# A fused retention and two-layer kernel: another order of products where two stages meet, keys and values loaded by pairs of batches, weights and queries requested later

## The chip, the core and the metric

One Trainium2 chip, one of its cores. The core has a matrix engine (TensorE: PE in the profile, and PEld for its weight loads), a vector engine (DVE), an activation engine (ACT), GpSimd (POOL), and SyncE (SP), which here only issues DMA requests, in program order, each after its own wait. The metric is the device time in microseconds of one execution. The kernel before takes 644.52 us (median of 4 runs, 644.33 to 644.72).

## What is computed

```python
# q, k, v: (4 batches, 8 heads, 768 tokens, 64), fp32
for t in range(S):
    state = gamma * state + outer(k[t], v[t])       # per batch and head
    y[t] = scale * q[t] @ state
x = y as (3072, 512)
h = x @ w_in                                        # 512 -> 2048
out = max(0.01 * h, h) @ w_out                      # 2048 -> 512
```

The recurrence is computed by chunks of 128 tokens: products inside a chunk (scores of queries and keys, masked, times values) and products of the queries with the state that is carried over. w_in and w_out arrive as 64-bit numbers and are turned into fp32 on ACT and DVE.

## The kernel before

There are NC = 6 chunks `c` of 4 batches `b`. The hidden dimension is cut into NU = 4 units `u`. For a chunk and a unit, `hidden` makes h and `output` adds its part of the result; both are done with seven block products instead of eight (M1 to M7), whose sums and differences are formed on DVE and copied on ACT. Each of the M products is a step of a generator (`seven`), so that other work can be put between two steps: `products(steps, n)` runs n of them.

The program has three parts. Chunks 0 and 1 are computed while the 64 weight pieces are still being loaded and converted (up to about 203 us of the trace). The last four raw pieces (60 to 63) lie in the two slots of the tag `qk` (60 and 62) and the two of `kv` (61 and 63); a slot can be loaded anew when DVE has read its piece. Meanwhile sums of the unit tiles are formed and stored to DRAM (`keep_unit`, line 1017, tensor `kept`). A middle part (lines 1059 to 1092) places the first visits of chunk 2 by hand among the steps of chunk 1. Then comes the main loop over n = 0 to 15, that is chunks 2 to 5 with four units each. There each chunk's inputs are treated once more by seven products: `inner` (line 1154) computes one unit's products in two groups, group 0 with the streamed weights `wa` and group 1 with `wb`, each a single buffer that `load_unit` (lines 1044 to 1049) fills from `kept`.

`inner` runs M1, M5, M4, M6, M2, M3, M7 (line 1163) in four banks of PSUM. M6 and M7 go to the bank that ACT fills with a copy of M1 (line 1167), so M6 waits for that copy; M3 goes to the bank of M5 and waits for its copy (line 1169); M7 waits for the copy of M6 (line 1173). `outer` (group 1) adds the parts on DVE (line 592) and applies the leaky function on ACT, four instructions (line 1198), each after its sum.

Two of the four iterations of a chunk hold a visit of the next chunk, for two batches at a time. `scores_of_pair` computes scores of queries and keys (line 357), then products of keys and values for the state (line 368). `joint_visit` computes the products of queries and state (line 413) and of weights and values (line 430). Before that, `decay_v` on POOL (line 142) multiplies the values by the powers of gamma.

Who loads what, on SP, in order:

- `end_mantissas`, after the last piece: `load(2, 0)`, `load(2, 1)`; each asks for queries with keys of a batch (line 121, 512 KB), then for keys and values (line 137, 512 KB).
- `next_heads`, after the visit of chunk 2: for each of two batches queries, then values, then keys (line 314, 256 KB each).
- `joint_visit`: values of two batches, keys of two batches, then `ahead`, the queries of the chunk after; and behind it `load_unit(n + 2, 0)`, the next `wa`.

A tile named `kv` of one batch holds keys and values side by side; the tag has two slots (`AHEAD = 2`), so a pair of batches uses both until its `joint_visit` has read the values.

The order where the middle part meets the main loop is written out at lines 1232 to 1245: the last output of chunk 1 is a generator `last` of seven steps, and `last` M1, M5, M6, M2; the scores of (3, 0); `last` M7; `inner(0, 0)`, `outer(0, 0)`; `last` M3 and M4; `inner(0, 1)`, `outer(0, 1)`; and the loop begins with `differences` (DVE) and `inner(1, 0)`.

Of the kernel before, what the change touches and what calls it, by code (L numbers as in the profile page):

```python
# [22 lines left out]
def kernel(  # L23
# [82 lines left out]
    def place_for(c, b, place=None):  # L106

        if place is None:
            x = work.tile([128, 2, HP, C], FP32, tag="qk", bufs=AHEAD, name=f"qk_{c}_{b}")
            y = work.tile([128, 2, H, D], FP32, tag="kv", bufs=AHEAD, name=f"kv_{c}_{b}")  # L110
        else:
            flat = place.rearrange("p i k n -> p (i k n)")
            half = 2 * HP * C
            if place.shape[1] == 7:
                rooms[b] = flat[:, 2 * half : 2 * half + 2 * HP * D]
            x = flat[:, 0:half].rearrange("p (s a t) -> p s a t", s=2, a=HP)
            y = flat[:, half : 2 * half].rearrange("p (s h d) -> p s h d", s=2, h=H)
        heads[c, b] = x, y
# [7 lines left out]
    def load_k(c, b):  # L126
        nc.sync.dma_start(out=heads[c, b][1][:, 0], in_=kv[c, b][:, 0])

    rooms = {}

    def spare(b):
        return lambda: rooms[b].rearrange("p (n a d) -> p n a d", n=2, a=HP)

    def load(c, b, place=None):
        place_for(c, b, place)
# [1 line left out]
        nc.sync.dma_start(out=heads[c, b][1], in_=kv[c, b])  # L137

    def decay_v(c, b, engine=nc.gpsimd):
        v = heads[c, b][1][:, 1]  # L140
        if engine is not nc.scalar:
            engine.tensor_tensor(out=v, in0=v,
                                 in1=gk[c].unsqueeze(2).to_broadcast([128, H, D]), op=ALU.mult)
        else:
            for h in range(H):
                engine.activation(v[:, h], v[:, h], AF.Identity, scale=gk[c][:, h : h + 1])
# [148 lines left out]
    def ahead(c, b):  # L295

        if c >= NC:
            return
        if b < 2:
            x = work.tile([128, 2, HP, C], FP32, tag="qk", bufs=AHEAD, name=f"qk_{c}_{b}")  # L300
        else:
            if b == 2:
                room[c] = new_o(0).rearrange("p i k n -> p (i k n)")
            x = room[c][:, ds((b - 2) * 2 * HP * C, 2 * HP * C)]
            x = x.rearrange("p (s a t) -> p s a t", s=2, a=HP)
        heads[c, b] = [x, None]
        load_qk(c, b)

    def load_kv(c, b, kinds):
        if heads[c, b][1] is None:  # L310
            heads[c, b][1] = work.tile([128, 2, H, D], FP32, tag="kv", bufs=AHEAD,
                                       name=f"kv_{c}_{b}")
        for i in kinds:
            nc.sync.dma_start(out=heads[c, b][1][:, i], in_=kv[c, b][:, i])

    room = {}

# [26 lines left out]
    def scores_of_pair(c, b, banks=None, mid=None):  # L344

        if b == 0 and c > JOINED:
            next_gq()
        banks = banks or bank
        at = [banks[j].rearrange("p (b m i t) -> p b m i t", b=2, m=HP // 2, i=2)
              for j in range(2)]  # L350
        sums = [banks[2 + h].rearrange("p (b a d) -> p b a d", b=2, a=HP) for h in range(2)]
        for n in range(2):
            x = heads[c, b + n][0]
            for m, i, a in quads:
                for h in range(2):
                    for j in range(2):
                        nc.tensor.matmul(at[j][ts(h, 64), n, m, i],  # L357
                                         lhsT=x[ts(j, 64), 1, a, ts(h, 64)],
                                         rhs=x[ts(j, 64), 0, a, ts(h, 64)],
                                         start=(n == 0 and a == 0), stop=True,  # L360
                                         skip_group_check=True)
        last = c == NC - 1
        for n in range(2):
            y = heads[c, b + n][1]
            for a in range(HP):
                for j in range(2):
                    for h in range(1 if last else 2):
                        nc.tensor.matmul(sums[h][ts(j, 64), n, a], lhsT=y[ts(h, 64), 0, 2 * a + j],  # L368
                                         rhs=y[ts(h, 64), 1, 2 * a + j],
                                         start=(n == 0 and a == 0), stop=True,  # L370
                                         skip_group_check=True)
        weights = scores[c, b] = []
        for j in range(2):
            am = work.tile([128, 2, HP // 2, 2, C // 2], FP32, tag=f"am{j}", name=f"am{j}_{c}_{b}")
            nc.vector.tensor_tensor(
                out=am.rearrange("p b m i t -> p (b m i) t"),
                in0=at[j].rearrange("p b m i t -> p (b m i) t"),
                in1=mask[:, 0].unsqueeze(1).to_broadcast([128, 2 * HP, C // 2]), op=ALU.mult)
            weights.append(am)
        p = b // 2  # L380
        old = state_of[p]
        free_again[p] = [old]
        if mid is None:
            mid = halves_of_states.pop(0)
            free_again[p].append(mid)
        plus(mid, old, sums[0])
        if not last:
            state_of[p] = halves_of_states.pop(0)
            plus(state_of[p], mid, sums[1])
        mid_of[p] = old, mid  # L390

    def rows_free(mm):

# [4 lines left out]
    def joint_visit(c, b, banks=None):  # L398
# [23 lines left out]
            return mm  # L422

        def value(n, crossed, after=None):
            y = heads[c, b + n][1]
            for m in range(HP // 2):
                for i in range(2):
                    for j in range(2):
                        h, a = j ^ crossed, 2 * m + i
                        mm = nc.tensor.matmul(at[n][j][ts(i, 64), m, ts(h, 64)],  # L430
                                              lhsT=y[ts(h, 64), 1, 2 * a + j],
                                              rhs=weights[j][ts(h, 64), n, m, i],
                                              start=(n == 1 and crossed == 1 and m == 0),
                                              stop=True, skip_group_check=True)
# [20 lines left out]
        for n in range(2):  # L455
            heads.pop((c, b + n))
        if later is not None:
            for n in range(2):
                load_kv(later[0], later[1] + n, (1,))
            for n in range(2):  # L460
                load_kv(later[0], later[1] + n, (0,))
            for n in range(2):
                decay_v(later[0], later[1] + n)
        for n in range(2) if c > JOINED else ():
            ahead(c + 1, b + n)

    def pair_of_banks(name):

# [65 lines left out]
    def end_mantissas():  # L534
# [4 lines left out]
            load_piece(n + 4 if n < 3 else n + 3)  # L539
        if n == N_PIECES - 1:  # L540
            new_pair(2)
            for b in range(AHEAD):
                load(2, b)
        if n % 4 == 3 and n > 7:
            add_sums(n // 4)

# [487 lines left out]
    def at_of(n):  # L1034
        return 2 + n // NU, n % NU
# [21 lines left out]
        load_unit(0, 1)  # L1057

    def next_heads():
        for b in range(2):  # L1060
            ahead(3, b)
            load_kv(3, b, (1, 0))
        for b in range(2):
            decay_v(3, b)

# [2 lines left out]
        (1, 1): dict(s2=[sum_of_unit(0, 2)], s5=[sum_of_unit(0, 3)]),  # L1068
        (0, 2): dict(s2=[sum_of_unit(1, 2)], s5=[sum_of_unit(1, 3)]),
        (1, 2): dict(s0=[keep_unit(1)], s2=[sum_of_unit(2, 0)]),  # L1070
        (0, 3): dict(s0=[lambda: load(2, 3, place_of_unit(2, "in23"))],
                     s4=[lambda: load(2, 2, place_of_unit(0, "in22"))],
                     s5=[sum_of_unit(3, 0)], s6=[sum_of_unit(3, 1), early_decays(2, 2)]),
        (1, 3): dict(s0=[begin_x(2), early_scores(2, 2, spare(3))],
                     s1=[sum_of_unit(3, 2)], s2=[sum_of_unit(3, 3)],
                     s3=[keep_unit(3)], s4=[early_visit(2, 2)],
                     s6=[early_decays(2, 0)]),
# [4 lines left out]
        (1, 1): dict(s6=[sum_of_unit(1, 1)]),  # L1082
        (0, 2): dict(s2=[sum_of_unit(2, 1)], s5=[sum_of_unit(2, 2)]),
        (1, 2): dict(s0=[sum_of_unit(2, 3)], s1=[keep_unit(2)]),
        (0, 3): dict(s0=[begin_units, early_scores(2, 0, spare(2))],
                     s1=[lambda: differences(*parts[1][1:])],
                     s3=[early_visit(2, 0), differ(2), next_heads],
                     s6=[sums(2, 0)]),
# [64 lines left out]

    def inner(n, group, held=False):

        c, u = at_of(n)
        w, count = streamed[group], 4 - group
        moving = operands(c, group)
# [2 lines left out]
        for m, q, j, s in INNER:  # L1161
# [16 lines left out]
            elif m == "M7":  # L1178
                plus(sums[:, 3], sums[:, 3], ps[3])
                plus(sums[:, 2], sums[:, 2], ps[3])  # L1180
        if not held:
            load_unit(n + 1, group)

# [54 lines left out]
    sums_of_x(2, 1)  # L1238
    inner(0, 0)
    outer(0, 0)  # L1240
    products(last, 2)
    inner(0, 1)
    outer(0, 1)

    for n in range(N2):
# [7 lines left out]
        if n + 1 < N2 and u == NU - 1:  # L1253
            sums_of_x(c + 1, 1)
        if n + 1 < N2:
            inner(n + 1, 0, held=visiting)
            outer(n + 1, 0)
        if visiting and u == 0:
            xs[c + 1] = new_x(c + 1)
        if visiting:  # L1260
            joint_visit(c + 1, 2 * u)
            load_unit(n + 2, 0)
        steps = output(c, os[c], [gs.pop(n)], u == 0, u == NU - 1, room=room if more else last_room,
                       order=FUSED if more else LAST)
        products(steps, 3)
        if c + 1 < NC and u < 2 and following(c + 1, 2 * u):
            scores_of_pair(*following(c + 1, 2 * u))
        products(steps, 1)
        if c + 1 < NC and u == 1:
            differences(*xs[c + 1])  # L1270
# [1 line left out]
            sums_of_x(c + 1, 0)  # L1272
        if more:
            inner(n + 1, 1)
            products(steps, 1)
            outer(n + 1, 1)
        if n + 2 == N2:
# [29 lines left out]
def _layout(q, k, v, w_in, w_out):  # L1307
# [15 lines left out]

    qk = np.stack([dims_first(q), dims_first(k)], axis=3).reshape(NC, B, 2 * D, 2, HP, C)
    kv = np.stack([tokens_first(k), tokens_first(v)], axis=3).reshape(NC, B, C, 2, H, D)
    DM, DF = w_in.shape

    w_in = w_in.reshape(H // 4, 2, 2, D, DF).transpose(2, 0, 1, 3, 4).reshape(DM, DF)
# [41 lines left out]
```

## Time and profile before

| | us |
|---|---|
| median of 4 runs | 644.52 (644.33 to 644.72) |
| profiled execution, its own time | 644.45 |
| its span, first to last instruction | 642.7 |
| PE busy | 633.0 (98%) |
| DVE busy | 460.9 (72%) |
| ACT busy | 269.5 (42%) |
| POOL busy | 22.2 (3%) |
| mean granted clock of TensorE | 0.997 |
| chain that ended last, on PE | 94% |
| longest groups on PE: line 648, bank from g and w | 89.9 |
| line 1163, bank from x and wb | 77.9 |

The span is 1.75 us shorter than the execution's own time; what lies outside it is taken as fixed. The "chain of work" view goes back from the last instruction to whatever released each step. The "timeline" view gives start, duration, engine, line, tiles and, in brackets, the idle time before an instruction and what ended it. In the DMA view of a stretch, the first row gives the busy share of the 16 DMA engines in 40 slices, the second what they moved.

### The profile page before, as it was taken

The page shows a single profiled execution, that of the slowest core. Times are in us where ns is not written, and L with a number is a line of the kernel's source. Part 1 is how long each engine was busy: PE and PEld are TensorE (multiplying, and loading weights), DVE is VectorE, ACT ScalarE, POOL GpSimd, SP SyncE. Part 2 cuts the span into 40 slices and gives each one's busy share as a digit, 9 for nine tenths or more (in the row PEclk, how much of TensorE's full clock was granted, in tenths as well). Part 3 has the DMA queues.
Part 4 walks back from the last instruction along what each step waited for, and adds up shares of the span by engine and source line. Part 5 has one row for each costly group of instructions (what it writes and reads, how often), then busy time and mean ns, then how long its engine had stood idle before and what let it go on. Part 6 is the DMA issues. An engine that isn't in the chain of part 4 may idle for free.

```text
span 642.7 us, 14314 instructions
## 1 busy us (share of the span) xinstructions
PE 633.0 (98%) x6086; PEld 571.4 (89%) x6086; DVE 460.9 (72%) x760; ACT 269.5 (42%) x515; POOL 22.2 (3%) x45
## 2 busy tenths in 40 slices
PE   8999999999999998999999999999999999999997
PEld 5888888888888887998999999999999999999996
DVE  5689769889979967466876746768637778637656
ACT  5876557257252134252342433523424323433521
POOL 2000000000011010101000001000010000000000
PEclk9999999999999999999999999999999999999999
DMA  8931327455964977547544584645455336545201
GB/s 335 406 116 47 117 66 244 137 196 153 309 252 134 339 292 234 182 152 248 153 134 135 191 276 130 204 157 160 152 183 188 98 115 188 165 145 172 86 1 67
DMA packets 89265, 113.43 MB, mean 176 GB/s; under 512 B 3432, under 2 KB 71912, under 8 KB 89200
## 3 DMA queue, kind: packets, MB, share of 16 engines
q1 hardware_dynamic: 88896, 111.88, 53.1%
q8 instruction: 48, 0.79, 0.5%
q10 hardware_dynamic: 304, 0.62, 0.3%
q14 instruction: 17, 0.14, 0.1%
HBM read 93.35 MB, written 19.14 MB: 175 GB/s over the span
## 4 chain that ended last, share of the span: by engine, by line
PE 94%; DMA 2%; ACT 1%; DVE 1%; issue 0%; SPq 0%; POOL 0%; DVEq 0%; POOLq 0%
PE bank L648 31%; PE bank L1163 27%; PE C_h L648 4%; PE A_h L648 4%; PE C_o L648 4%; PE A_o L648 4%; PE B_h L648 4%; PE B_o L648 4%; PE D_o L648 2%; PE D_h L648 2%; PE d L669 2%; DMA kv<-in_kv_dram 1%; PE bank L430 1%; PE bank L413 1%; PE bank L368 1%; PE bank L357 1%
## 5 line engine op out<-in xcount | busy, mean ns | idle before, releaser
L592 DVE TENSOR_TENSOR made<-made,bank 128x512 f32<-128x512 f32 (+1 forms) x96 | 56.4, 618 | 62.1 <-PE bank L1163 57.6
L592 DVE TENSOR_TENSOR o<-o,bank 128x512 f32<-128x512 f32 (+2 forms) x91 | 58.6, 661 | 53.7 <-PE bank L648 32.9
L648 PE MATMUL bank<-g,w 128*128 128x256 f32 x384 | 89.9, 382 | 0.0
L1163 PEld LDWEIGHTS bank<-x,wb 128*128 128x128 f32 x672 | 77.6, 192 | 1.6 <-issue 0.8
L648 PEld LDWEIGHTS bank<-g,w 128*128 128x128 f32 x384 | 70.7, 190 | 9.2
L1163 PE MATMUL bank<-x,wb 128*128 128x128 f32 x672 | 77.9, 275 | 0.6 <-issue 0.6
L1163 PE MATMUL bank<-x,wa 128*128 128x128 f32 x512 | 69.6, 278 | 2.9 <-ACT bank L1167 2.9
L1163 PEld LDWEIGHTS bank<-x,wa 128*128 128x128 f32 x512 | 64.4, 193 | 4.7 <-ACT bank L1167 3.9
L648 PE MATMUL bank<-gd,w 128*128 128x256 f32 x288 | 66.1, 379 | 0.0
L648 PEld LDWEIGHTS bank<-gd,w 128*128 128x128 f32 x288 | 54.7, 190 | 7.4
L1163 PE MATMUL bank<-t,wa 128*128 128x128 f32 x384 | 54.5, 279 | 0.0
L1198 ACT ACTIVATE g<-g 128x512 f32<-128x512 f32 x64 | 39.4, 631 | 34.2 <-DVE g L592 34.2
L1163 PEld LDWEIGHTS bank<-t,wa 128*128 128x128 f32 x384 | 49.2, 196 | 0.0
L1167 ACT COPY bank<-bank 128x512 f32<-128x512 f32 (+1 forms) x32 | 16.7, 522 | 66.4 <-PE bank L1163 66.1
L592 DVE TENSOR_TENSOR g<-made 128x512 f32<-128x512 f32 x64 | 42.7, 688 | 1.2
L741 ACT COPY bank<-bank 128x512 f32<-128x512 f32 x17 | 9.7, 570 | 72.6 <-PE bank L648 72.5
L595 DVE TENSOR_TENSOR gd<-g,gd 128x512 f32<-128x512 f32 x48 | 33.2, 692 | 4.9
L759 ACT COPY bank<-bank 128x512 f32<-128x512 f32 x16 | 9.1, 570 | 47.0 <-PE bank L648 47.0
L648 PE MATMUL bank<-g,last 128*128 128x256 f32 x120 | 28.3, 380 | 0.0
L648 PE MATMUL bank<-gd,last 128*128 128x256 f32 (+1 forms) x124 | 27.5, 373 | 0.0
L648 PE MATMUL A_h<-x,w 128*128 128x256 f32 x112 | 26.6, 380 | 0.0
L648 PEld LDWEIGHTS bank<-gd,last 128*128 128x128 f32 x124 | 22.9, 190 | 3.3 <-DVE gd L595 0.3
(222 smaller groups left out, 1027.4 us busy)
## 6 DMA issues: line engine op xcount, KB each, us to landing
wa<-kept SPq DMA_DIRECT2D x16, 1344.0 KB, 7.8
raw<-in_weights_dram SPq DMA_DIRECT2D x31, 512.0 KB, 4.3
wb<-kept SPq DMA_DIRECT2D x16, 896.0 KB, 5.3
kv<-in_kv_dram SPq DMA_DIRECT2D x28, 256.0 KB, 4.7
wa<-kept SPq DMA_DIRECT2D x16, 448.0 KB, 5.2
wb<-kept SPq DMA_DIRECT2D x16, 448.0 KB, 6.1
out_dram<-o SPq DMA_DIRECT2D x23, 256.0 KB, 3.9
kept<-w SPq DMA_DIRECT2D x12, 448.0 KB, 6.2
```

Of the source, the lines that this page charges most:

```text
L357: nc.tensor.matmul(at[j][ts(h, 64), n, m, i], lhsT=x[ts(j, 64), 1, a, ts(h, 64)], rhs=x[ts(j, 64), 0, a, ts(h, 64)], start=(n == 0 and a = ...
L368: nc.tensor.matmul(sums[h][ts(j, 64), n, a], lhsT=y[ts(h, 64), 0, 2 * a + j], rhs=y[ts(h, 64), 1, 2 * a + j], start=(n == 0 and a == 0), s ...
L413: mm = nc.tensor.matmul(at[n][j][ts(i, 64), m, ts(h, 64)], lhsT=by_half[h][ts(j, 64), n, a], rhs=x[ts(j, 64), 0, a, ts(h, 64)], start=(n = ...
L592: nc.vector.tensor_tensor(out=out, in0=a, in1=b, op=ALU.add)
L595: nc.vector.tensor_tensor(out=out, in0=a, in1=b, op=ALU.subtract)
L648: nc.tensor.matmul(to, lhsT=block(w, sa)[:, k, ts(i, 128)], rhs=rhs[:, k, a:z], start=(first and (i == 0 or split) and n == 0 and k == 0), ...
L669: nc.tensor.matmul(banks[r][:, i, :], lhsT=block(2 * u, r + 2 * kh)[:, k, ts(i, 128)], rhs=x[:, 2 * kh + th, k, :], start=(step == 0 and i ...
L741: nc.scalar.copy(out=bank_of("B"), in_=ps)
L759: nc.scalar.copy(out=bank_of("D"), in_=ps)
L1163: nc.tensor.matmul(ps[q][:, i], lhsT=w[:, j, i], rhs=part_of(moving[i], s), start=(i == 0 and m in ("M1", "M5", "M4")), stop=True, skip_gr ...
L1167: nc.scalar.copy(out=ps[3], in_=ps[0])
L1198: nc.scalar.activation(g[:, i], g[:, i], AF.Prelu, alpha=0.01)
```

## The change

Three things are done. First, keys and values of chunks 2 to 5 lie differently in DRAM (a host-side reordering) and come in two loads for a pair of batches, one of the values and one of the keys, each of 512 KB, into tiles of their own (`of_pair`). The keys of the pair after are requested at the end of `scores_of_pair`, the values still in `joint_visit`. Second, requests change their order: after the last piece, values and keys of (2, 0) and (2, 1) come first, then the two loads of queries; `next_heads` does the same for chunk 3; in the loop `load_unit(n + 2, 0)` comes behind `scores_of_pair`, and `ahead` behind `inner(n + 1, 1)`. Third, at the junction `last` M4 moves behind `inner(0, 1)`, and the first step of `inner(1, 0)` with its copy is issued ahead of `outer(0, 1)`; the other steps stay behind `differences`.

```diff
+    def of_pair(c, b, kind, place=None):
+        if place is None:
+            place = work.tile([128, 2, H, D], FP32, tag="kv", bufs=AHEAD,
+                              name=f"{'kv'[kind]}_{c}_{b}")
+        for n in range(2):
+            (keys, vals)[kind][c, b + n] = place[:, n]
+        nc.sync.dma_start(out=place, in_=kv[c, b + kind])
...
@@ scores_of_pair, at its end
+        if following(c, b) is not None and c > JOINED:
+            of_pair(*following(c, b), 0)
@@ joint_visit, at its end
         if later is not None:
-            for n in range(2):
-                load_kv(later[0], later[1] + n, (1,))
-            for n in range(2):
-                load_kv(later[0], later[1] + n, (0,))
+            of_pair(*later, 1)
             for n in range(2):
                 decay_v(later[0], later[1] + n)
-        for n in range(2) if c > JOINED else ():
-            ahead(c + 1, b + n)
@@ end_mantissas, after the last piece
-            for b in range(AHEAD):
-                load(2, b)
+            for b in range(2):
+                heads[2, b] = [work.tile([128, 2, HP, C], FP32, tag="qk", bufs=AHEAD,
+                                         name=f"qk_2_{b}")]
+            of_pair(2, 0, 1)
+            of_pair(2, 0, 0)
+            for b in range(2):
+                load_qk(2, b)
@@ next_heads
+        of_pair(3, 0, 1)
+        of_pair(3, 0, 0)
         for b in range(2):
             ahead(3, b)
-            load_kv(3, b, (1, 0))
@@ middle part: the loads of (2, 2) and (2, 3), same places
-        (0, 3): dict(s0=[lambda: load(2, 3, place_of_unit(2, "in23"))],
-                     s4=[lambda: load(2, 2, place_of_unit(0, "in22"))],
+        (0, 3): dict(s0=[early_inputs(2, 2, 1, 2)],
+                     s4=[early_inputs(2, 2, 0, 0)],
@@ inner
     def inner(n, group, held=False):
+        products(inner_steps(n, group, held), 8)
+
+    def inner_steps(n, group, held=False):
...
+            yield
@@ the junction
     inner(0, 0)
     outer(0, 0)
-    products(last, 2)
+    products(last, 1)
     inner(0, 1)
+    products(last, 1)
+    begun = inner_steps(1, 0, held=True)
+    products(begun, 1)
     outer(0, 1)
@@ the loop
-            inner(n + 1, 0, held=visiting)
+            if n == 0:
+                products(begun, 7)
+            else:
+                inner(n + 1, 0, held=visiting)
             outer(n + 1, 0)
...
             joint_visit(c + 1, 2 * u)
-            load_unit(n + 2, 0)
         steps = output(...)
         products(steps, 3)
         if c + 1 < NC and u < 2 and following(c + 1, 2 * u):
             scores_of_pair(*following(c + 1, 2 * u))
+        if visiting:
+            load_unit(n + 2, 0)
...
             inner(n + 1, 1)
+            for i in range(2) if visiting else ():
+                ahead(c + 2, 2 * u + i)
@@ host layout
+    new = kv[JOINED:].reshape(NC - JOINED, B // 2, 2, C, 2, H, D).transpose(0, 1, 4, 3, 2, 5, 6)
+    kv[JOINED:] = new.reshape(kv[JOINED:].shape).copy()
```

More of the change, by code (lines that the diff above doesn't have):

```diff
@@ L113, in place_for @@
             half = 2 * HP * C
-            if place.shape[1] == 7:
-                rooms[b] = flat[:, 2 * half : 2 * half + 2 * HP * D]
             x = flat[:, 0:half].rearrange("p (s a t) -> p s a t", s=2, a=HP)
@@ L127, in load_k, with early_inputs, do, spare @@
         nc.sync.dma_start(out=heads[c, b][1][:, 0], in_=kv[c, b][:, 0])
-    rooms = {}
-    def spare(b):
-        return lambda: rooms[b].rearrange("p (n a d) -> p n a d", n=2, a=HP)
+    keys, vals, rooms = {}, {}, {}
+    def of_pair(c, b, kind, place=None):
[5 more added lines that the diff above has]
+        nc.sync.dma_start(out=place, in_=kv[c, b + kind])
+    def early_inputs(c, b, kind, k):
+        def do():
+            place = place_of_unit(k, f"in{c}{b}_{kind}")
+            flat = place.rearrange("p i k n -> p (i k n)")
+            half = 2 * HP * C
+            heads[c, b + kind] = [flat[:, 0:half].rearrange("p (s a t) -> p s a t", s=2, a=HP)]
+            load_qk(c, b + kind)
+            of_pair(c, b, kind, flat[:, half : 2 * half].rearrange(
+                "p (n h d) -> p n h d", n=2, h=H))
+            rooms[kind] = flat[:, 2 * half : 2 * half + 2 * HP * D]
+        return do
+    def spare(kind):
+        return lambda: rooms[kind].rearrange("p (n a d) -> p n a d", n=2, a=HP)
     def load(c, b, place=None):
@@ L139, in decay_v @@
     def decay_v(c, b, engine=nc.gpsimd):
-        v = heads[c, b][1][:, 1]
+        v = vals[c, b] if c >= JOINED else heads[c, b][1][:, 1]
         if engine is not nc.scalar:
@@ L305, in ahead @@
             x = x.rearrange("p (s a t) -> p s a t", s=2, a=HP)
-        heads[c, b] = [x, None]
+        heads[c, b] = [x]
         load_qk(c, b)
[L309 to L314, printed above, removed]
     room = {}
@@ L363, in scores_of_pair @@
         for n in range(2):
-            y = heads[c, b + n][1]
+            key, val = keys.pop((c, b + n)), vals[c, b + n]
             for a in range(HP):
@@ L367, in scores_of_pair @@
                     for h in range(1 if last else 2):
-                        nc.tensor.matmul(sums[h][ts(j, 64), n, a], lhsT=y[ts(h, 64), 0, 2 * a + j],
-                                         rhs=y[ts(h, 64), 1, 2 * a + j],
+                        nc.tensor.matmul(sums[h][ts(j, 64), n, a], lhsT=key[ts(h, 64), 2 * a + j],
+                                         rhs=val[ts(h, 64), 2 * a + j],
                                          start=(n == 0 and a == 0), stop=True,
@@ L424, in value @@
         def value(n, crossed, after=None):
-            y = heads[c, b + n][1]
+            val = vals[c, b + n]
             for m in range(HP // 2):
@@ L430, in value @@
                         mm = nc.tensor.matmul(at[n][j][ts(i, 64), m, ts(h, 64)],
-                                              lhsT=y[ts(h, 64), 1, 2 * a + j],
+                                              lhsT=val[ts(h, 64), 2 * a + j],
                                               rhs=weights[j][ts(h, 64), n, m, i],
@@ L1070 @@
         (1, 2): dict(s0=[keep_unit(1)], s2=[sum_of_unit(2, 0)]),
-        (0, 3): dict(s0=[lambda: load(2, 3, place_of_unit(2, "in23"))],
-                     s4=[lambda: load(2, 2, place_of_unit(0, "in22"))],
+        (0, 3): dict(s0=[early_inputs(2, 2, 1, 2)],
+                     s4=[early_inputs(2, 2, 0, 0)],
                      s5=[sum_of_unit(3, 0)], s6=[sum_of_unit(3, 1), early_decays(2, 2)]),
-        (1, 3): dict(s0=[begin_x(2), early_scores(2, 2, spare(3))],
+        (1, 3): dict(s0=[begin_x(2), early_scores(2, 2, spare(1))],
                      s1=[sum_of_unit(3, 2)], s2=[sum_of_unit(3, 3)],
@@ L1084 @@
         (1, 2): dict(s0=[sum_of_unit(2, 3)], s1=[keep_unit(2)]),
-        (0, 3): dict(s0=[begin_units, early_scores(2, 0, spare(2))],
+        (0, 3): dict(s0=[begin_units, early_scores(2, 0, spare(0))],
                      s1=[lambda: differences(*parts[1][1:])],
```

## The prediction

> **What bounds the kernel now.** I read the page's busy times first:
>
> ```profile
> PE 633.0 (98%) x6086; PEld 571.4 (89%) x6086; DVE 460.9 (72%) x760; ACT 269.5 (42%) x515; POOL 22.2 (3%) x45
> ```
>
> TensorE works 98% of the span, and the change takes no product away. So it can only win where PE stands still or runs slowly, and lose by making it stand still elsewhere. The view of waits for PE alone shows the places worth naming behind the start-up:
>
> ```profile
> PE bank L1163 <- ACT bank L1167: 2.9, 1, 2.9
> ...
> PE bank L368 <- POOL kv L142: 0.6, 1, 0.6
> ```
>
> The largest is at the junction, in `inner(1, 0)`. The timeline from 249 to 261 us:
>
> ```profile
> 251.69 1.23 ACT L1198 ACTIVATE g<-g 128x512 f32<-128x512 f32 x2 [2.71 <-DVE g L592]
> ...
> 254.76 0.58 ACT L1167 COPY bank<-bank 128x512 f32<-128x512 f32 x1
> ...
> 255.39 1.78 PE L1163 MATMUL bank<-x,wa 128*128 128x128 f32 x10 [2.90 <-ACT bank L1167]
> ...
> 256.96 1.49 PE L1163 MATMUL bank<-t,wa 128*128 128x128 f32 x6
> ```
>
> The copy of M1 stands on ACT behind the four leaky functions of `outer(0, 1)`, which wait for DVE; M6 waits for the copy. Six products then take 1.49 us at 256.96; the same six take 0.83 us further on, at 260.02. The windows view says why; its columns are PE, PEld, DVE, ACT, POOL busy, then the granted clock:
>
> ```profile
> 252.80:256.20 3.40, 0.81 (x7) 0.81 (x8) 3.16 (x6) 2.71 (x6) 0.00 (x0) 1.00 0.90 281
> 256.20:259.60 3.40, 3.40 (x19) 3.40 (x18) 0.78 (x2) 1.31 (x3) 0.00 (x0) 0.50 0.01 3
> ```
>
> A stretch in which PE worked 0.81 of 3.40 us is followed by one at half clock, which costs 3.4 / 2 = 1.7 us more. The stall is thus worth 4.6 us: M1 starts at 249.64, the visit behind `inner(1, 0)` at 260.79, 11.15 us for what takes 6.25 (the same x56 at 235.41 in the chain). That is 4.9 with small gaps.
>
> The Trainium skill ("TensorE: Matmul & The Clock Gate", HAM oscillation) gives the rule that idle gaps of PE above about 3.4 us bring the clock down. Here 2.90 us did. By the rule the junction would be worth 2.9 us only, and a new gap of 3 us would cost nothing beyond itself; the row decides, and I count the clock.
>
> The second place is the scores of (3, 0), timeline from 226 to 236 us:
>
> ```profile
> 230.59 1.16 PE L357 MATMUL bank<-qk 64*64 64x64 f32 x64
> ...
> 231.69 1.04 POOL L142 TENSOR_TENSOR kv<-kv,dec 128x512 f32<-128x512 f32 x1 [1.56 <-DMA kv<-in_kv_dram]
> ...
> 232.79 0.69 PE L368 MATMUL bank<-kv 64*64 64x64 f32 x32 [0.56 <-POOL kv L142]
> ```
>
> The last values land just late. Why, SP's timeline and the DMA view from 202 to 235 us say:
>
> ```profile
> 184.58 0.33 SPq L137 DMA_DIRECT2D kv<-in_kv_dram  x1
> 198.86 0.33 SPq L121 DMA_DIRECT2D qk<-in_qk_dram  x1
> 202.67 0.33 SPq L137 DMA_DIRECT2D kv<-in_kv_dram  x1
> 203.05 3.48 SPq L1017 DMA_DIRECT2D kept<-sums  x4
> ```
> ```profile
> DMA  0196899999999999988999999999999999999841
> GB/s 0 35 119 124 289 397 421 417 413 405 368 341 346 356 312 304 336 201 279 352 348 364 332 349 375 366 328 340 367 384 407 397 392 400 385 395 385 315 147 62
> ```
>
> From about 205 to 233 us the DMA engines are full, one request behind the other. Whatever is put in at 203 us delays all behind it.
>
> **The junction.** In the new order M1 of `inner(1, 0)` still starts at 249.64 (old clock), since the same products precede it. What changes is ACT: the M1 copy is ready one M after the start, as in `inner(0, 0)` (M1 235.25, copy 236.34), so at 250.73 to 251.30, and M6, due at 249.64 + 3 x 0.9 = 252.35, does not wait. DVE has `last` M4's sum in front of `outer(0, 1)`: it needs M4 (249.64) and starts at 249.9, so the first sum comes at 250.6, against 250.97 now. The leaky functions end at 254.4 instead of 254.85. But the copies of M5, M4 and M6 stay behind them: M5's at 254.33 to 254.91, M6's at 255.33 to 255.92. M3, due at 254.15, waits 0.8 us for the first, M7 0.1 for the last. `inner` ends at 256.9 instead of 260.79: **3.9 us gained**, by bounds 3.0 (a sum later on DVE) to 4.9 (no wait). A gap of 0.8 is near the 0.56 at 232, which kept the clock.
>
> **The requests at 203 us.** This part speaks against the change. The four slots for (2, 0) and (2, 1) become free with the last four pieces: SP shows 181.71 and 198.86 for `qk`, 184.58 and 202.67 for `kv`. Now both `kv` tiles are asked for first. The values take the slot of 184.58 (the one taken first today); the keys wait for 202.67, and both queries, whose slots have been free since 181.71 and 198.86, stand behind them on SP. So 2 x 512 KB move into the full stretch, 1.05 MB at the 415 GB/s of its first slices: 2.5 us for all behind it (stores of `kept`, `wa`, `wb`, the loads of chunk 3).
>
> First effect: the scores of (2, 0), line 357 at 208.43. Requests of 512 KB took 3.6, 3.8 and 4.6 us to land (198.86, 234.92, 202.67), two in a row land 1.25 us apart. Keys land at 206.3 to 207.3, queries at 207.5 to 208.5 and 208.8 to 209.8; the second is due at 208.92. Stall 0 to 1.0, I take 0.8. It is not added, since the next one swallows it.
>
> Second effect: the scores of (3, 0). The trace's landings of the four half-megabytes behind `wb` are 228.29, 229.64, 230.92 and 232.33. With 2.5 us more, less 0.1 for longer rows, they are 230.8, 232.1, 233.3 and 234.7, and the queries are now the last two. Line 357, due at 231.4, gets its first half at 233.3 and its second at 234.7; 0.5 us for that half, 1.05 for line 368 (values decayed by 233.0): the next product starts at 236.3 instead of 233.42, **2.9 us lost**, the present 0.77 us of that place already within it. Bounds: 0.3 (the order alone, no backlog) and 4.1 (values in the backlog too, 0.52 MB more).
>
> Does this gap, 1.9 and 0.8 us with half a microsecond of work between, halve the clock? Rows: 2.59 us idle of a 3.4 us stretch did, 0.56 did not. This one puts 1.7 to 2.7 us in one stretch. 0 to 1.7 us; I take 0 for the forecast and make the other a rival of nearly equal weight.
>
> **The visits in the loop.** At (4, 0) line 368 loses 0.30 us at 297.66 to keys landing at 297.52; keys now come a visit earlier. In `inner`, PE stands still for 0.57 us at 302.17 for nothing the view of waits shows ("issue"), and the weights' group is 0.83 us longer than its like; a 16 KB fetch of instructions (the queue "instruction") began at 300.18, late, in a stretch full of keys, queries and `wa`. With these spread out, I count **1.1 us gained**, bounds 0 and 1.2.
>
> Values of two batches now land together before the first decay. From an idle DMA 512 KB take 3.6 to 4.6 us, two decays 2.1: ready 5.7 to 6.7 after the request. Line 368 comes 6.4 after it (262.75 to 269.17), its second half 0.5 later. Nothing, at worst 0.3 in each of five visits. `wa` is asked for at 270.3, not 266.0, behind 512 KB of keys: 8.7 us to land when alone (316.59 to 325.31) plus 1.25 is 280.3; it is due at 281.92. Nothing, 1.6 us of cover; beyond it each microsecond counts in four visits. Queries, asked for at 277 or so, are due a visit later. POOL's decays keep their place, and only DMA waits are queued behind SP's new waits.
>
> **Sum**, on the profiled execution (644.45, that is 642.7 and 1.75 around it; 0.07 below the median): +2.9 - 3.9 - 1.1 = -2.1, **642.4 us** on the median's scale. From chunk 3 on PE has no wait left but 0.27 us four times, which nothing here touches.
>
> **Rivals.**
> - *The clock falls at the scores of (3, 0).* For: 1.7 to 2.7 us idle in one stretch; against: work between the two halves. 642.4 + 1.7 = 644.1.
> - *The queries are in time* (SP's order does not bind or the backlog is absorbed by the slice at 201 GB/s). 0.3 - 3.9 - 1.1 = -4.7: 639.8.
> - *The backlog is longer*: the values get the later slot as well, or instruction fetches join the queue. For: fetches already came late in this stretch. 4.1 + 1.7 (clock) - 3.9, and the 1.1 not won: +1.9, 646.4. Slower than before from the point where the queries of (3, 1) land after 236.8 us, or after 235.1 with the clock halved.
> - *The junction does not do what it says*: the M5 copy, still behind the leaky functions, keeps M3 waiting over 2 us and the clock falls there too. 2.9 - 1.0 - 1.1 = +0.8: 645.3.
>
> **Chances.** Forecast 0.36, clock 0.24, queries in time 0.13, longer backlog 0.19, junction 0.08. What measurement tells from no change is 0.2%, 1.3 us: faster means below 643.2, slower above 645.8. Faster: 0.30 + 0.05 + 0.13 = 0.48. Slower: 0.02 + 0.15 + 0.02 = 0.19. Within: 0.33. The range goes from 639.3, below the case of queries in time, to 646.5, just beyond the longer backlog.
>
> **What would show it.** After: no wait for line 1167 at the junction, but one of 0.8 us for line 1169; clock 1.00 there; two queries issued right behind the keys at 202.67; line 357 at the scores of (3, 0) waiting for queries, 3 us in all; no gap near 298 and 302. I am wrong if line 357 does not wait, or if `wa` ends a wait in a visit.

## The result and the profile after

After: 644.25 us, the median of 45 runs (641.76 to 648.14). Before, run beside it on the same chips: 645.5 us, the median of 71 (641.94 to 653.59). The ratio is 0.9977, 95% interval 0.9966 to 0.9987: 1.5 us faster (2.2 to 0.8), where the forecast was 2.1. The level was off too: the four runs of before shown at first (644.52) lay 1.0 us below what 71 give, so 642.4 was too low by that alone.

The profiled execution of after took 644.96 us, span 643.0, against 644.45 and 642.7. The page's line of busy times:

```profile
PE 632.5 (98%) x6086; PEld 570.9 (89%) x6086; DVE 462.4 (72%) x760; ACT 269.3 (42%) x515; POOL 22.9 (4%) x45
```

The same 6086 products, the same 98%: only gaps and clock have moved. The view of waits for PE (line 369 is 357 before, 1182 is 1163, 1188 is 1169):

```profile
PE bank L369 <- DMA qk<-in_qk_dram: 2.3, 2, 1.8
PE ap L369 <- DMA qk<-in_qk_dram: 1.3, 2, 0.8
...
PE bank L1182 <- ACT made L1188: 0.6, 1, 0.6
```

The 2.9 us for ACT at the junction are gone, with the wait for M5's copy in their place, and the scores now wait for queries in two places: 2.3 us at (3, 0), 1.3 at (2, 0). SP's timeline shows the order of the requests:

```profile
185.88 0.33 SPq L136 DMA_DIRECT2D v<-in_kv_dram  x1
203.13 0.33 SPq L136 DMA_DIRECT2D k<-in_kv_dram  x1
203.51 1.72 SPq L119 DMA_DIRECT2D qk<-in_qk_dram  x2
```

Both queries stand behind the keys, whose slot comes free at 203. PE's timeline at the scores of (3, 0):

```profile
230.82 1.89 PE L662 MATMUL bank<-g,last 128*128 128x256 f32 x8
234.50 0.69 PE L369 MATMUL bank<-qk 64*64 64x64 f32 x32 [1.79 <-DMA qk<-in_qk_dram]
235.73 1.13 PE L369 MATMUL bank<-qk 64*64 64x64 f32 x32 [0.54 <-DMA qk<-in_qk_dram]
236.64 1.93 PE L380 MATMUL bank<-v,k 64*64 64x64 f32 x64
238.50 2.03 PE L662 MATMUL bank<-g,last 128*128 128x256 f32 x8
```

The 64 products of line 380 take 1.93 us, where line 368 took 1.11 (269.17 before). The windows view (PE, PEld, DVE, ACT, POOL busy, clock, DMA share, GB/s) says why:

```profile
231.80:235.20 3.40, 1.60 (x37) 1.01 (x35) 0.69 (x1) 0.00 (x0) 2.04 (x2) 1.00 1.02 399
235.20:238.60 3.40, 2.87 (x97) 2.75 (x97) 1.29 (x2) 0.00 (x0) 0.00 (x0) 0.50 0.66 251
```

PE worked 1.60 of 3.40 us, 47%, and the next stretch ran at half clock, though no idle gap was longer than 1.79 us. The next product starts at 238.50. In before it was:

```profile
233.42 1.99 PE L648 MATMUL bank<-g,last 128*128 128x256 f32 x8
```

This execution was 0.46 us late at 192 already; the place cost 4.6.

The junction, PE's timeline, before (first product and visit) and after:

```profile
249.64 0.39 PE L1163 MATMUL bank<-x,wa 128*128 128x128 f32 x2
...
260.79 0.46 PE L430 MATMUL bank<-am,kv 64*64 64x64 f32 x16
```

```profile
254.77 0.38 PE L1182 MATMUL bank<-x,wa 128*128 128x128 f32 x2
...
259.98 0.49 PE L1182 MATMUL bank<-x,wa 128*128 128x128 f32 x2 [0.58 <-ACT made L1188]
...
262.04 0.46 PE L444 MATMUL bank<-am,v 64*64 64x64 f32 x16
```

From M1 to the visit 7.27 us instead of 11.15: 3.9 gained, with the clock at full speed throughout. The visits in the loop gain 1.16: 0.32 at the scores of (4, 0), whose keys are now in time, and 0.83 in the group of `wb` behind them. There before has two pieces and after one:

```profile
300.11 2.06 PE L1163 MATMUL bank<-x,wb 128*128 128x128 f32 x17
302.74 3.06 PE L1163 MATMUL bank<-x,wb 128*128 128x128 f32 x25 [0.57 <-issue]
```
```profile
301.04 4.85 PE L1182 MATMUL bank<-x,wb 128*128 128x128 f32 x42
```

So in this execution +4.6 - 3.9 - 1.16 = -0.4, and 0.5 at the start: the two profiles are level at 311 us (0.09 apart), and the span of after is 0.3 us longer at the end, while by the medians after is 1.5 us faster. One execution is not enough here, because the granted clock differs between executions of one kernel: in 22 of the 87 of before that ran beside the experiments it was full to the end (mean 0.999 or more; median 644.9 us), in 46 it was 0.996 to 0.998 (645.8), in 19 lower (647.9). After has, of the 46 executions whose clock is on record, 23 at full clock (642.9), 18 at 0.996 to 0.998 (645.0), 5 lower (646.3). Nor is the clock all: both profiles have one stretch at half clock while PE works, but that of before is a short one for its clock (644.45, median 645.8) and that of after is not (644.96, median 645.0).

### The profile page after: what moved, and what is told of

It reads as the page before. It is cut to its first block, busy times and chain, and to the rows that moved or that the text cites. A ratio compares the mean times of both kernels' runs of the same rounds, so it can differ in the third digit from the quotient of the medians.

```text
span 643.0 us, 14287 instructions
## 1 busy us (share of the span) xinstructions
PE 632.5 (98%) x6086; PEld 570.9 (89%) x6086; DVE 462.4 (72%) x760; ACT 269.3 (42%) x515; POOL 22.9 (4%) x45
## 4 chain that ended last, share of the span: by engine, by line
PE 90%; DMA 4%; DVE 3%; ACT 2%; issue 1%; SPq 1%; DVEq 0%
PE bank L662 31%; PE bank L1182 27%; PE B_o L662 4%; PE C_o L662 4%; PE A_o L662 4%; PE A_h L662 3%; PE C_h L662 3%; PE B_h L662 3%; DMA qk<-in_qk_dram 2%; PE D_o L662 2%; PE d L683 2%; PE D_h L662 2%; DMA raw<-in_weights_dram 1%; PE bank L444 1%; PE bank L369 1%; PE bank L380 1%
```

## The experiments

The theory: the junction gains some 3 to 4 us; the requests at 203 us put a megabyte too much ahead of `wa`, `wb` and the loads of chunk 3, and the queries stand last in a full queue, so PE waits and the clock falls. The rivals: the parts only work together; the order of the requests counts and not their bytes; the clock's fall has nothing to do with the gap. Each kernel's ratio is to before on the same chip.

| kernel | us | ratio, 95% interval | executions at full clock |
|---|---|---|---|
| after | 644.25 | 0.9977, 0.9966 to 0.9987 | 23 of 46 |
| e1 junction alone | 642.97 | 0.9952, 0.9933 to 0.9971 | 12 of 12 |
| e2 requests alone | 647.3 | 1.0030, 1.0005 to 1.0056 | 3 of 12 |
| e3 queries first | 642.28 | 0.9939, 0.9916 to 0.9962 | 6 of 12 |
| e4 e5 with early copies | 642.44 | 0.9948, 0.9929 to 0.9968 | 6 of 12 |
| e5 e3 with `wb` later | 638.89 | 0.9897, 0.9875 to 0.9919 | 4 of 4 |
| e6 gap filled | 643.99 | 0.9972, 0.9952 to 0.9991 | 8 of 12 |
| e7 asked later alone | 645.38 | 0.9991, 0.9971 to 1.0010 | 3 of 12 |
| e8 `wb` later alone | 640.9 | 0.9924, 0.9904 to 0.9944 | 5 of 5 |
| e9 gap filled more | 644.28 | 0.9977, 0.9960 to 0.9994 | 11 of 12 |
| e10 keys in the visit | 648.52 | 1.0040, 1.0018 to 1.0062 | 4 of 12 |
| e11 keys last | 642.65 | 0.9966, 0.9943 to 0.9988 | 9 of 12 |

### The junction alone (e1)

Before, with the junction's new order and nothing else:

```diff
-    products(last, 2)
+    products(last, 1)
     inner(0, 1)
+    products(last, 1)
+    begun = inner_steps(1, 0, held=True)
+    products(begun, 1)
     outer(0, 1)
...
-            inner(n + 1, 0, held=visiting)
+            if n == 0:
+                products(begun, 7)
+            else:
+                inner(n + 1, 0, held=visiting)
```

> The kernel before with the junction part of the change alone (last M4 behind inner(0, 1), the first step of inner(1, 0) and its copy ahead of outer(0, 1)); loads as before. Theory: the junction gains what the prediction said, inner(1, 0) takes 7.3 us from its first product to the visit behind it and not 11.15, no half clock there; nothing else moves, so about 3.9 us less than the kernel before (ratio 0.994), and the waits at 297 and 302 us are still there. Rival: the junction by itself gains only the clock's share, about 1.7 us (0.997), since M3 waits for the copy of M5 instead.

3.1 us faster (1.9 to 4.3). M1 to the visit takes 7.28 us, as in after. Its waits:

```profile
PE bank L1167 <- issue: 1.0, 1, 1.0
...
PE bank L1167 <- ACT made L1173: 0.6, 1, 0.6
```

The "issue" gap near 300 and the late values stay, as they should. All 12 executions run at full clock, against 22 of 87 of before: there it was the junction's stall that lowered it.

### The requests alone (e2)

After, with the junction's old order (the edit of e1 backwards).

> The changed kernel with the junction of the kernel before; all load parts of the change stay. Theory: the queries behind the keys of the last slot cost 3.0 to 3.4 us at the scores of (3, 0), plus about 1.2 to 1.7 us in executions in which the clock falls there, less 1.1 us won at the first visits: 1.9 to 3.6 us slower than before (ratio 1.003 to 1.0055), with the stall at the junction as before. Rival: the load parts as a whole are neutral (1.000), and the changed kernel lost its gain within the junction.

1.9 us slower (0.3 to 3.6). The junction's -3.1 and this +1.9 give -1.2; both together measured -1.5. The parts add up, and the requests are a loss. Its windows at the scores of (3, 0):

```profile
231.20:234.60 3.40, 1.30 (x7) 0.80 (x5) 1.06 (x2) 0.00 (x0) 1.83 (x2) 1.00 1.03 335
234.60:238.00 3.40, 2.04 (x64) 1.85 (x68) 0.00 (x0) 0.00 (x0) 0.21 (x1) 0.51 0.75 291
238.00:241.40 3.40, 3.40 (x78) 3.01 (x73) 2.60 (x4) 0.00 (x0) 0.00 (x0) 0.50 0.31 56
```

The queries landed later still (235.77 and 237.05), so two stretches in a row had much idle time, and two ran at half clock.

### Queries first (e3), keys last (e11), and `wb` later (e8)

Three ways to undo part of the requests, all in after. e3, behind the last piece of chunk 1:

```diff
+            load_qk(2, 0)
             of_pair(2, 0, 1)
+            load_qk(2, 1)
             of_pair(2, 0, 0)
-            for b in range(2):
-                load_qk(2, b)
```

Each request now stands at the time its slot comes free, so that at 203 us only the keys are put in, as 512 KB, and not 1.5 MB. e11, in the loads of chunk 3:

```diff
         of_pair(3, 0, 1)
-        of_pair(3, 0, 0)
         for b in range(2):
             ahead(3, b)
+        of_pair(3, 0, 0)
```

e8 moves the three lines that make and load `wb` from `begin_units` to a place behind these loads.

> The changed kernel with one thing altered: after the last weight piece the four requests stand in the order in which their slots come free (queries of (2, 0), values, queries of (2, 1), keys). Theory: no wait for queries at the scores of (2, 0), and the backlog of 1.05 MB at 203 us is gone, so the scores of (3, 0) wait 0.3 to 1.0 us instead of 2.3 and the clock stays up: 3 to 4.5 us less than the changed kernel, 639.5 to 640.5 us by the scale of the prediction (ratio to before 0.992 to 0.994). Rival: the order within the loads of chunk 3 (queries last) is what costs; then the wait of 2 us stays and the ratio stays near 0.998.

> The changed kernel with the loads of chunk 3 in the order values, queries, keys. Theory (backlog): the queries land 1.25 us sooner, the scores of (3, 0) wait about 1.2 us less for them, but line 380 then waits for the keys, the last to land; the gain is 0.5 to 0.8 us, and fewer executions lose the clock: ratio 0.995 to 0.997. Rival of the order: queries in front of the keys settle it, the wait goes but for 0.3 us and the ratio is 0.993.

> The changed kernel with one thing altered: the first load of wb (1.3 MB) is asked for behind the loads of chunk 3, so that much of the full stretch no longer stands in front of the queries. Theory of the backlog: the queries of (3, 0) land about 3.5 us sooner (1.38 MB at 390 GB/s), before their use, so the scores of (3, 0) hardly wait (0 to 0.5 us) though the queries of (2, 0) still come late and still cost 1 to 1.3 us at the scores of (2, 0): 2.5 to 3 us less than the changed kernel, 0.994 of before. Rival: it is the order of the requests on SP, not the bytes, that makes the queries late; then the wait of 2 us stays.

All three are faster than after: e3 by 0.9939 / 0.9977, 2.5 us; e8 by 3.4; e11 by 0.7, which the intervals don't part. In e3 `inner(0, 0)` starts at 235.63 (240.37 in after, 235.25 before): 0.4 us, near the 0.3 that the prediction gave as the lower bound, "the order alone, no backlog". In e8, with the 1.3 MB of `wb` (896 and 448 KB) no longer ahead of them, the queries land at 228.75 and 230.09 instead of 234.45 and 235.69, and the scores run without a break (PE's timeline up to 233 us, so the second line has 38 of its 64 products):

```profile
231.39 1.16 PE L369 MATMUL bank<-qk 64*64 64x64 f32 x64
232.37 0.85 PE L380 MATMUL bank<-v,k 64*64 64x64 f32 x38
```

In e11 the wait is shared out, 0.8 us for a query and 0.6 for the keys.

So the order within the last four loads moves little, and bytes ahead of them move much: the rival "order, not bytes" falls. What stays open is e3's clock: 6 of its 12 executions lose some of it (643.5 against 640.2 us), and its profile, taken at full clock, doesn't show where.

### Both, and copies ahead of the leaky functions (e5, e4)

e5 is e3 with e11's order and e8's later `wb`. e4 has, beyond that, the copies of M5, M4 and M6 ahead of the last two leaky functions of `outer(0, 1)`:

```diff
-    outer(0, 1)
+    ending = outer_steps(0, 1)
+    products(ending, 1)
+    products(begun, 3)
+    products(ending, 1)
...
-                products(begun, 7)
+                products(begun, 4)
```

> As e3 (the four requests after the last piece in the order in which their slots come free), and for chunk 3 values, queries, keys, with the first load of wb (1.3 MB, needed at 248 us) behind them; the junction as in the change. Theory: the two waits for queries that e3 still showed at the scores of (3, 0), 0.9 us together, go, and wb still lands before its use: 0.7 to 1.3 us less than e3, ratio to before 0.991 to 0.993. Rival: the wait only moves, to wb at inner(0, 1) or to the keys, and the time is that of e3 (0.994).

> As e3, and further: for chunk 3 values, then queries, then keys; the first load of wb (1.3 MB, needed at 248 us) asked for behind them; at the junction the copies of M5, M4 and M6 ahead of the last two leaky functions. Theory: no wait at the scores of (3, 0) (0.7 us less than e3) and no wait for the copy of M5 (0.6 us less): 638.5 to 639.3 us, ratio 0.990 to 0.992. Rival: wb then comes late for inner(0, 1), or the leaky functions come late for output, and a new wait takes it back.

e4 writes over parts that `outer(0, 1)` still reads, so unit 0's output of chunk 2 is changed. e5 is the fastest kernel of the study: 638.89 us, 6.6 faster than before (5.2 to 8.1), and its interval lies wholly below that of after. Of the three waits shown of after only that for M5's copy (line 1188, 0.6 us) is left.

e4, which was to take it away, is 3.3 us slower than e5 by the ratios. Its waits:

```profile
PE bank L427 <- DVE made L606: 1.8, 1, 1.8
PE bank L444 <- ACT made L1194: 1.2, 1, 1.2
```

A miss: products and copies went ahead, and now the visit waits for the rest of ACT's and DVE's work, 3.0 us instead of 0.6. The work in front of the visit had not become less, only the wait had moved to its end.

### Filling the gap (e6, e9)

After with 9 (e6) and 16 (e9) products ahead of the scores of (3, 0) that the computation doesn't need:

```diff
+    for _ in range(16):
+        fill(0)
     scores_of_pair(3, 0)
```

> The changed kernel with nine short products of no use (2 us of PE) put in front of the scores of (3, 0), where PE waits for the queries; their results are overwritten. Theory: the wait for data is the same, but PE is not idle, so the clock is never halved there: the executions at mean clock 0.996 go, and nearly all runs lie with the undisturbed ones of the changed kernel, 642.5 to 643.5 us where that kernel has half its runs at 645; ratio to before 0.996 at most. Rival: the slower half of the runs has another cause than this gap; then the two groups stay as they were and the nine products change nothing or cost up to 0.3 us.

> As e6, with sixteen products of no use instead of nine (3.5 us of PE), since in the profile of e6 the queries came 1.6 us after the nine had ended and the clock fell all the same. Theory: PE now has work over the whole wait, so no execution loses the clock there; all runs at 0.999 or more, between 643 and 644.5 us (the sixteen end up to 1 us after the queries have come). Rival: the slower half of the runs of the changed kernel has another cause; then runs at 0.997 remain in like number.

e6 settles nothing: in its profile the queries landed at 236.09 and 237.34, 1.6 us later than in after's, 1.6 us of idle time stayed, and the clock fell. In e9 the filler outlasts the queries (its timeline of PE):

```profile
231.88 3.62 PE L695 MATMUL bank<-mask 128*128 128x512 bf16 x16
235.43 1.39 PE L369 MATMUL bank<-qk 64*64 64x64 f32 x64
236.64 1.17 PE L380 MATMUL bank<-v,k 64*64 64x64 f32 x64
```

11 of 12 executions now keep the full clock, against 23 of 46. The time is that of after, because the filler costs what the clock gives back: executions at full clock take 644.2 instead of 642.9. This idle gap is what lowers the clock in half of the executions of after; that rival falls as well.

### Asked later alone (e7)

Before, with weights and queries asked for later in the program, as in the change:

```diff
-        for n in range(2) if c > JOINED else ():
-            ahead(c + 1, b + n)
...
-            load_unit(n + 2, 0)
...
+        if visiting:
+            load_unit(n + 2, 0)
...
+            for i in range(2) if visiting else ():
+                ahead(c + 2, 2 * u + i)
```

> The kernel before with only the later requests in the loop: load_unit(n + 2, 0) behind scores_of_pair, ahead behind inner(n + 1, 1); keys and values in four loads as before, the junction as before. Theory of the instruction fetch: the gap of 0.6 to 1.0 us in inner(1, 1) or so, near 302 us, goes, since the fetch no longer stands behind 2.8 MB of queries and wa; the stall at the junction stays: 0.8 to 1.1 us less than before, ratio 0.9985. Rival: the gap comes from the keys and values alone, or from the density of instructions, and stays; ratio 1.000.

No difference to be measured, and the "issue" gap stays (0.9 us). SP's timeline shows that for `wa` the edit did not do what it says; only the queries moved:

```profile
290.99 2.13 SPq L314 DMA_DIRECT2D kv<-in_kv_dram  x4
293.16 0.52 SPq L1042 DMA_DIRECT2D wa<-kept  x1
```

`wa` is still asked for right behind the values and keys, since SP has nothing ahead of it to wait for. In after the request for keys stands there, waiting for line 380, and holds `wa` back.

### Keys asked for in the visit (e10)

After, with the keys' request moved from the end of the scores into the visit, behind the values:

```diff
-        if following(c, b) is not None and c > JOINED:
-            of_pair(*following(c, b), 0)
...
             of_pair(*later, 1)
+            of_pair(*later, 0)
```

> The changed kernel with the keys of the next pair asked for in joint_visit, right behind the values, and not at the end of scores_of_pair; so SP no longer waits for line 380 before it asks for wa, and wa is on its way some 6 us sooner. Theory: keys, and wa behind them, fill the DMA engines right after the visit; the instruction fetch number 23 comes at 1.3 to 1.45 chunks behind its like (1.02 in the changed kernel) and the gap of 0.6 to 1.0 us in inner (n = 1) is back, 0.5 to 1.0 us slower than the changed kernel, ratio 0.9990. Rival: the two loads of 4 KB rows alone cleared the way; no gap, ratio 0.9977.

2.6 us slower than before (1.2 to 4.0), where after is 1.5 faster: a miss. The gap that the theory expected back near 300 us is not there, and neither theory had the cause. In the visit the values now take the slot that has been free since the scores, so they land a visit's length early, and POOL's decays of them start as the visit ends instead of 4.5 us later. The timeline of all engines in e10:

```profile
288.50 2.49 POOL L161 TENSOR_TENSOR v<-v,dec 128x512 f32<-128x512 f32 x2
288.56 1.53 DVE L605 TENSOR_TENSOR made<-made 128x512 f32<-128x512 f32 x1
...
290.12 1.41 DVE L605 TENSOR_TENSOR g<-made 128x512 f32<-128x512 f32 x1
...
291.93 1.78 PE L661 MATMUL bank<-gd,w 128*128 128x256 f32 x7 [0.85 <-DVE x L464]
```

and the same sum and decays in after:

```profile
291.28 0.69 DVE L606 TENSOR_TENSOR made<-made 128x512 f32<-128x512 f32 x1
...
295.71 2.04 POOL L161 TENSOR_TENSOR v<-v,dec 128x512 f32<-128x512 f32 x2 [4.51 <-DMA v<-in_kv_dram]
```

A DVE sum of 128x512 takes 1.53 and 1.41 us beside POOL's decays, 0.69 without them. What stands behind it on DVE, the scaling of the visit's results (line 464), comes late, and M5's products wait for it: 2.5 us in three visits. The rest of the 4.1 us between the two kernels is not shown by the profile, which is of one of the shortest executions; 8 of 12 had less than the full clock.

## Why the prediction was right or wrong

**The junction (-3.9): right in mechanism, and in size in the profile.** M1 to the visit went from 11.15 to 7.27 us, M3 waits 0.58 us for M5's copy (0.8 forecast). Over all executions the junction alone is worth 3.1 (1.9 to 4.3). Of the forecast 3.9, 1.7 was the half clock behind the stall, counted as if it fell once in each execution; in 22 of 87 of before the clock stays full, and there the junction is worth 644.9 - 643.0 = 1.9, near the 2.2 that remain without the clock. In the 46 at 0.996 to 0.998 it is worth 2.8, in the 19 lower ones 4.9.

**The scores of (3, 0) (+2.9): the step that failed, in two ways, both of size.** In the profile the place cost 4.6 us. The cause was as forecast: queries behind the keys at 203 us, the backlog carried on to the loads of chunk 3, the order there adding little (e11) and the bytes much (e3, e8).
- "I take 0 for the forecast": the clock did fall in the profiled execution, which cost 1.2 us, and e9 shows that this gap is what lowers it in half of the executions. Those at full clock take 642.9, the others 645.0. So two of the cases in the prediction came true side by side, the forecast's and its first rival, "the clock falls": taken from the 645.5 of the 71 runs, they are 643.4 and 645.1. A median between them is no case of its own.
- The backlog was worked out as 2.5 us, from 1.05 MB at 415 GB/s, and was 3.1: with the 0.46 us of the start taken off, the four half-megabytes behind `wb` landed 2.9 to 3.2 us later than those in the same places before, and so did the first store of `kept` (212.06 against 208.35). The queries were worked out to land at 233.3 and 234.7 and landed at 234.45 and 235.69, 0.7 and 0.5 late. The DMA view of after, 202 to 240 us in 40 slices, has 250 and 168 GB/s from 206.8 to 208.7, while the queries were moving; why it is so little there is not shown.

```profile
GB/s 0 0 121 362 414 250 168 331 411 419 396 419 389 356 326 340 295 278 141 196 293 357 379 376 384 371 326 320 366 399 410 410 397 388 405 403 311 140 43 56
```

The two make up the 1.7 us between 2.9 and 4.6. The prediction's own break-even fits: with the clock halved it put the loss of the whole gain at queries landing after 235.1, and less 0.46 they landed at 235.23. The stall at the scores of (2, 0) came to 1.3 us, above its bounds of 0 to 1.0; it was swallowed by the later wait, as expected.

**The visits in the loop (-1.1): right, 1.16.** The "issue" gap stays in e1 and e7, where the loads come as before, and is gone in the kernels with the new loads. That a late fetch of instructions caused it is inferred, not shown: in the traces of before, e1 and e7 the fetch starts 10.0 to 10.2 us behind the one ahead of it, in after 7.3; but in e10 it is 9.6, and there is no gap. The two edits priced at nothing, values in pairs and `wa` later, end no wait in the view of after.

**The rivals.** "Queries in time" is what e8 and e5 made of the change, not what the change did. "The longer backlog" came true in part: 3.1 us and not 2.5, though the values kept the earlier slot (185.88). "The junction doesn't do what it says" fell with e1.

**The sum.** -2.1 was forecast, -1.5 measured, with the forecast just within the interval (2.2 to 0.8). That the two are so near is in part luck. By the medians the junction brings 3.1 (3.9 forecast), and the requests with the visits cost 1.9 alone (e2) and 1.6 behind the new junction (after against e1), near the forecast +2.9 - 1.1 = +1.8, although the clock, which the forecast left out, is in them. At full clock alone they cost nothing: 642.9 in after, 643.0 in e1. Where that is made up for stays open: the profiled executions of before and of e1 (641.11, median 642.97) are 1 to 2 us shorter than ordinary ones at their clock, so what the old loads cost in an ordinary execution is in no profile here. The absolute time was 1.0 us off besides, with the four runs of before.

## What to carry to other kernels

Put requests into a queue in the order in which their slots come free, and look at what stands behind a request that waits: the same request later in the program comes no later in time unless something ahead of it waits (e7), and comes much too late if something does. In a stretch where the DMA engines are full, take away the bytes that are not needed yet before changing the order: moving one weight load behind the loads in need gained 3.4 us, the order among these 0.7 at most seen. Price a gap of PE together with the stretch around it, as a chance and not as a yes or no, and look at several executions before its half clock is counted either way.

## What the runs showed of the hardware

- The clock halves after a stretch of 3.40 us in which PE worked 1.60, in after, and 0.81, in before; the longest idle piece of the first was 1.79 us. In e2 a stretch at half clock in which PE worked 2.04 of 3.40 was followed by another, in after one with 2.87 by full clock. It falls in some executions of a kernel and not in others: 23 of 46 of after kept it. The Trainium skill ("TensorE: Matmul & The Clock Gate", HAM oscillation) names idle gaps above about 3.4 us; the gaps measured here are below that, and they decide. The same page (What's actually happening) has a window of 3413 ns that runs freely; the length agrees with the clock in the traces, whose half-clock stretches (the one that each program ends in left out) last 3.413 us in before, after and e6 and twice that, 6.827, in e2 and e7. That its running freely is why one execution keeps the clock and the next does not is not shown by any run here.
- DVE's sum of two tiles in SBUF took 1.53 and 1.41 us instead of 0.69 while POOL worked. The Trainium skill ("SBUF — State Buffer", Who interferes with whom) says that such a DVE instruction and a GpSimd one that reads SBUF exclude each other; the trace agrees: the sum is 0.84 us longer, and one decay takes 1.04.
